# Twelve token tiles' output rows summed in DRAM, one tile's first-norm sums on ScalarE, and a new order of the work

## The chip, the cores and the metric

The kernel runs on one core of a Trainium2 chip. The metric is the time of one execution in device microseconds, the median of several runs. The core has five engines that run side by side and wait for each other by semaphores: PE (TensorE, matmuls into PSUM), DVE (VectorE), ACT (ScalarE), POOL (GpSimd) and SP (SyncE). SP issues most of the transfers, POOL those that accumulate into their destination.

## What is computed

The input x is A_q, 2048 tokens of 640 numbers in bf16. Two branches are mixed by a gate of one number for each token:

```python
g = sigmoid((x * gate_w).sum(-1, keepdims=True))
# branch A: a convolution over the whole sequence
kv = shift_conv(A_k, A_shift_k) * A_v          # four taps along the tokens
y  = causal_conv(kv, A_ssm_k) + kv * A_ssm_D    # by rfft and irfft of length 4096
a  = x * y
# branch B: a mixer and an MLP
h  = gelu(layernorm(x) @ w1)                    # 640 -> 640
hs = token_shift(h) @ w2                        # four groups, shifted by 1, -1, 2, -2 tokens
x1 = x + hs
b  = x1 + gelu(layernorm(x1) @ w3) @ w4         # 640 -> 1536 -> 640
out = g * a + (1 - g) * b
```

## The kernel before

All data stand in one SBUF array ("arena" in the profile), and PSUM is one array of eight banks ("PSall"). Tokens come in 16 tiles of 128 rows; X[:, t, :] holds tile t of x and is overwritten step by step until it holds (1 - g) * h2 @ w4.

*The first norm* (ln1, L892) has two forms. For tiles below LNS = 10, DVE makes the statistics with two bn_stats and one aggregate (ln_bn). For the others ACT makes them in two passes over the 640 columns, a sum and a sum of squares, each with an accumulated output. DVE normalises the tile, and PE (first 8 tiles) or a DMA transposes it.

*Mixer and MLP.* mm1 and mm2 are the two products of the mixer; the residual of mm2 is added on DVE (L967), which frees the PSUM bank, and ACT squares the result for the second norm. mm3 makes the MLP's hidden layer 512 tokens at a time (sc = 0 to 3), and mm4(t) (L993) its output for one tile: 12 matmuls of 384 columns and 12 of 256, and then an identity matmul that adds X's last 256 columns.

*The convolution* goes over five chunks of 128 channels. Transforms along the sequence are matmuls with constant matrices, and unit(c) (L1004) multiplies the spectra: products and sums on DVE, some of the sums by accumulating transfers of POOL within SBUF, where the order's list ON says so. final(g, o, q, k) (L1025) transforms back and multiplies by g * x, for a pair k of token tiles (ta = 4o + q and tb = 4o + 3 - q) and a group of columns: group 0 is columns 0 to 383, group 1 columns 384 to 639. Pairs 0 to 7 are tiles (12, 15), (13, 14), (8, 11), (9, 10), (4, 7), (5, 6), (0, 3), (1, 2). Group 1 needs units 3 and 4, which are the last ones.

*How the output comes together.* Columns 0 to 383 (NA = 384) are summed in DRAM: base(t) (L988) scales x by 1 - g on ACT and SP writes it; mm4(t) scales its result on ACT, and POOL adds it to DRAM with an accumulating transfer (L1000); group 0 of final is added in the same way (L1047), one transfer of 256 rows of 768 bytes for a pair. Columns 384 to 639 are summed on the chip: the identity matmul adds x in mm4, group 1 of final multiplies (L1050), adds X (L1051), and SP writes the sum, 256 rows of 512 bytes (L1053); pairs 6 and 7 do this in two halves. Since transfers to the same rows must follow one another, POOL waits for the landing of one before it issues the next to the same place.

*The order.* Each operation is recorded with a number, in the order of the calls, and SEQUENCE gives the order in which they are handed out to the engines; each engine runs its own operations strictly in that order. PLACES names the PSUM bank of each accumulation, and a bank's next user waits for the last reader of the one before. The semaphore waits follow from both lists. At the end SP waits for every transfer that it hasn't seen land.

Of the kernel before, what the change touches and what calls it, by code (L numbers as in the profile page):

```python
# [433 lines left out]
def bass_gated_mix__ssm_conv_h3__mixer_s_mlp__prompt_kernel(  # L434
    nc, A_q, A_k, A_v, A_shift_k, A_ssm_k, A_ssm_D, B_x, B_w1, B_w2, B_w3, B_w4, gate_w, out,
):
    S, D, F = 2048, 640, 1536
    NT, DC, FC, NB = 16, 5, 12, 4
    GROUPS = ((0, 3), (3, 5))
    NA = 384  # L440
# [28 lines left out]
    def ps(n, cls):  # L469
# [3 lines left out]
    SEQUENCE = [27, 46, 2, 4, 1, 7, 45, 0, 5, 24, 3, 8, 47, 25, 48, 28, 9, 130, 26, 10, 11, 31, 53, 12, 52, 32, 13,  # L473
# [383 lines left out]
    def bn_math(t0, t1):  # L857
        for a, b in ((t0, t1),) if t0 >= 4 else ((t, t + 1) for t in range(t0, t1)):
            mean, var = bna[:, a:b, 0], bna[:, a:b, 1]
            if a >= LNS:  # L860
                tt(st[0, 4][:, a:b], mean, mean, ALU.mult)
                stt(st[0, 3][:, a:b], st[0, 1][:, a:b], 1e-5, st[0, 4][:, a:b], ALU.add, ALU.subtract)
            else:
                ts(st[0, 3][:, a:b], var, 1e-5, None, ALU.add)
# [286 lines left out]
```

## Time and profile before

| | before |
|---|---|
| median of 3 runs | 222.24 us (221.77 to 222.59) |
| the profiled execution | 222.23 us |
| its span | 220.3 us |
| PE busy | 209.6 us (95%), 1410 matmuls |
| DVE busy | 211.6 us (96%), 417 instructions |
| ACT busy | 193.2 us (88%), 324 instructions |
| POOL busy | 55.9 us (25%), 57 instructions |
| DMA queue of SP | 66.2% of 16 engines' span |
| DMA queue of POOL | 27.7% of 16 engines' span |

Span is the time from the first instruction of the profiled execution to its last. Busy PE counts matmuls in flight, which overlap. A line of the profile can be that of a helper: L646 is every tensor_tensor on DVE, L651 every tensor_scalar, L656 every operation of ACT, L678 every matmul, L237 every DMA. Idle time stands in brackets behind an instruction, with what ended it. The landing of a transfer is counted from its issue.

### The profile page before, as it was taken

To read this page: it belongs to the slowest core of one execution; us is meant where nothing else is said; L and a number is where in the kernel's file an instruction comes from. 1 tells how busy PE (TensorE), PEld (TensorE's weight loads), DVE (VectorE), ACT (ScalarE), POOL (GpSimd) and SP (SyncE) were. 2 spreads that over 40 slices of the span, in tenths; PEclk is the share of its full clock that TensorE was granted. 3 is DMA by queue.
4 is the path that set the end of the run, shared out by engine and by line. 5 is a ranking of instruction groups with operands and counts; after the bars stand their busy time and mean duration, and the time that the engine had idled before them with its cause. 6 is when DMAs were issued, how large, how long until landed. Compare 5 with 4: busy or idle time off the path is not lost.

```text
span 220.3 us, 3850 instructions
## 1 busy us (share of the span) xinstructions
PE 209.6 (95%) x1410; PEld 125.9 (57%) x1410; DVE 211.6 (96%) x417; ACT 193.2 (88%) x324; POOL 55.9 (25%) x57
## 2 busy tenths in 40 slices
PE   5999999899999999999999999999999999999970
PEld 2489865455675444765446575445667445677740
DVE  5999999999999979999999999999999999999993
ACT  2389999999999999999999999999977898566981
POOL 0432303300005100005140002054025427277431
PEclk9999999999999999999999999999999999999996
DMA  6997999999998999959979885699699969889896
GB/s 168 348 283 183 216 201 271 175 247 201 161 338 227 269 257 183 206 98 184 215 139 148 190 153 95 129 167 195 139 226 147 218 119 254 179 100 96 110 158 118
DMA packets 80561, 41.39 MB, mean 188 GB/s; under 512 B 59129, under 2 KB 77086, under 8 KB 80542
## 3 DMA queue, kind: packets, MB, share of 16 engines
q1 hardware_dynamic: 73872, 31.89, 66.2%
q0 software_dynamic: 6496, 9.18, 27.7%
q8 instruction: 11, 0.18, 0.3%
q10 hardware_dynamic: 174, 0.07, 0.1%
q14 instruction: 8, 0.07, 0.1%
HBM read 14.88 MB, written 5.77 MB: 94 GB/s over the span
## 4 chain that ended last, share of the span: by engine, by line
DVE 73%; DMA 10%; PE 10%; ACT 3%; issue 2%; SPq 0%
DVE arena L646 63%; PE PSall L678 10%; DMA arena<-arena 8%; DVE arena L847 3%; DVE arena L651 3%; ACT arena L656 3%; DVE arena L967 2%; DMA arena<-in_A_q_dram 2%; DVE arena L933 1%; DVE arena L848 0%; DVE arena L852 0%; SPq L237 0%; DVE arena L721 0%
## 5 line engine op out<-in xcount | busy, mean ns | idle before, releaser
L678 PE MATMUL PSall<-arena 128*128 128x512 bf16 (+5 forms) x1349 | 201.3, 310 | 3.3 <-DVE arena L646 2.0
L646 DVE TENSOR_TENSOR arena<-arena 128x1024 bf16<-128x1024 bf16 (+12 forms) x266 | 173.4, 716 | 2.0 <-DMA arena<-arena 1.1
L678 PEld LDWEIGHTS PSall<-arena 128*128 128x128 bf16 x1349 | 121.7, 98 | 82.4 <-DVE arena L646 2.9
L656 ACT ACTIVATE arena<-PSall 128x512 bf16<-128x512 f32 (+6 forms) x157 | 93.1, 664 | 11.0 <-PE PSall L736 4.9
L656 ACT ACTIVATE arena<-arena 128x640 bf16<-128x640 bf16 (+5 forms) x105 | 90.4, 890 | 2.1 <-DVE arena L646 1.8
L855 POOL TENSOR_TENSOR arena<-arena 128x2 f32<-128x2 f32 (+2 forms) x15 | 19.5, 1306 | 84.1 <-DVE arena L852 67.9
L237 POOL DMA_DIRECT2D out_dram<-arena x24 | 25.5, 1302 | 15.5 <-DVE arena L646 8.5
L656 ACT ACTIVATE arena<-PSall,arena 128x640 bf16<-128x640 f32 (+2 forms) x32 | 20.5, 657 | 8.6 <-PE PSall L678 8.6
L237 POOL DMA_DIRECT2D arena<-arena x14 | 12.3, 882 | 59.6 <-DVE arena L646 59.6
L651 DVE TENSOR_SCALAR arena<-arena 128x640 bf16<-128x640 bf16 (+6 forms) x37 | 13.2, 378 | 0.1
L967 DVE SCALAR_TENSOR_TENSOR arena<-PSall,arena 128x640 bf16<-128x640 f32 x16 | 12.7, 812 | 0.0
L847 DVE BATCH_NORM_STATS2 arena<-arena 128x6 f32<-128x320 bf16 x20 | 8.7, 478 | 1.8 <-DMA arena<-in_A_q_dram 1.8
L701 PE MATMUL PSall<-arena 128*128 128x512 bf16 x15 | 6.4, 589 | 2.2 <-DVE arena L698 2.2
L933 DVE TENSOR_SCALAR arena<-arena 32x256 bf16<-32x256 bf16 (+1 forms) x23 | 5.5, 237 | 0.3
L656 ACT ACTIVATION_READ_ACCUMULATOR arena<-arena 128x1 f32 x28 | 5.7, 204 | 0.0
L701 PEld LDWEIGHTS PSall<-arena 128*128 128x128 bf16 x15 | 1.8, 134 | 5.0 <-issue 2.8
L908 PE MATMUL PSall<-arena 128*128 128x128 bf16 x40 | 3.4, 220 | 0.2 <-DVE arena L651 0.2
L852 DVE SCALAR_TENSOR_TENSOR arena<-arena 128x2 f32<-128x2 f32 (+2 forms) x19 | 3.0, 159 | 0.0
L908 PEld LDWEIGHTS PSall<-arena 128*128 128x128 bf16 x40 | 2.4, 98 | 0.9 <-DVE arena L651 0.9
L704 ACT ACT_TABLE_LOAD x1 | 1.3, 1283 | 1.4 <-PEq L1136 1.4
L848 DVE BATCH_NORM_AGGREGATE arena<-arena 128x2 f32<-128x12 f32 x10 | 1.8, 199 | 0.0
L967 DVE DVE_READ_ACCUMULATOR arena<-PSall,arena 128x1 f32 x16 | 1.2, 76 | 0.0
(19 smaller groups left out, 2.9 us busy)
## 6 DMA issues: line engine op xcount, KB each, us to landing
arena<-arena POOLq DMA_DIRECT2D x9, 512.0 KB, 6.9
arena<-in_A_ssm_k_dram SPq DMA_DIRECT2D x5, 512.0 KB, 4.5
arena<-in_A_q_dram SPq DMA_DIRECT2D x6, 320.0 KB, 5.9
arena<-in_B_w_dram SPq DMA_DIRECT2D x1, 1920.0 KB, 14.0
out_dram<-arena SPq DMA_DIRECT2D x16, 96.0 KB, 2.9
out_dram<-arena POOLq DMA_DIRECT2D x16, 96.0 KB, 4.7
arena<-in_A_q_dram SPq DMA_DIRECT2D x8, 192.0 KB, 3.3
out_dram<-arena POOLq DMA_DIRECT2D x8, 192.0 KB, 4.4
```

What stands on the lines that cost most here:

```text
L237: fn = lambda e: e.dma_start(out, in_, **kw)
L646: P.op(eng, lambda e: e.tensor_tensor(o, real(a), real(b), op), [a, b], [o], dve_ns(o, [a, b], 2) if eng == "dve" else 500)
L651: P.op(eng, lambda e: e.tensor_scalar(o, real(a), s1, s2, op0=op0, **({} if op1 is None else {"op1": op1})), [a] + aps, [o], dve_ns(o, [a] ...
L656: P.op("act", lambda e: e.activation(real(o), real(a), f, bias=bias, scale=scale, **({"accum_out": accum} if accum is not None else {})), ...
L678: fns.append(lambda e, l=l, r=r, i=i: e.matmul(real(o), l, r, start=(i == 0), stop=(i == last)))
L701: P.op("pe", lambda e: e.matmul(real(pw), warm[:, 0:128], warm[:, 128:640], start=True, stop=True), [warm], [pw], 427.0 if i < 14 else 216.0)
L847: P.op("dve", lambda e, o=o, i=i: e.bn_stats(o, i), [i], [o], 400)
L852: P.op("dve", lambda e: e.scalar_tensor_tensor(o, a, x, b, op0=op0, op1=op1), [a, b] + aps, [o], n_of(o) / 0.96 + 65)
L855: P.op("pool", lambda g: g.tensor_tensor(o, a, e, ALU.pow), [a, e], [o], dur)
L908: P.op("pe", [lambda e, c=c, pb=pb, xn=xn: e.transpose(real(pb)[:, 128 * c:128 * (c + 1)], xn[:, 128 * c:128 * (c + 1)], ident) for c in r ...
L933: P.op("dve", lambda e, o=hT[q, 4, c0:c0 + n], i=hx[q, :]: e.tensor_scalar(o, i, 1.0, None, op0=ALU.mult), [hx[q, :], *near], [hT[q, 4, c0 ...
L967: P.op("dve", lambda e: e.scalar_tensor_tensor(x, real(pr), 1.0, x, op0=ALU.mult, op1=ALU.add, accum_out=st[1, 0][:, t:t + 1]), [pr, x], [ ...
```

## The change

DRAM_PAIRS names pairs 0 to 5, that is tiles 4 to 15. For these, all 640 columns are summed in DRAM: base scales and writes 640 columns in place of 384, mm4 drops the identity matmul and its accumulating transfer has 640 columns, and group 1 of final drops the addition of X; its product goes to DRAM by an accumulating transfer of POOL where SP wrote the sum before. Tiles 0 to 3 (pairs 6 and 7) stay as they are. POOL so has six transfers more and SP six fewer, and the bytes that POOL adds for twelve tiles of mm4 grow by two thirds.

In the first norm, tile 3 joins tiles 10 to 15, whose sums ACT makes. Its two bn_stats, its aggregate and one small operation on DVE become two passes on ACT and two small operations on DVE.

SEQUENCE and PLACES are new. Beside the operations that come and go, SP's and POOL's own orders stay; on PE 8, on ACT 21 and on DVE 31 operations stand elsewhere in their engine's list. On DVE the read of mm2 for tile 5 comes eight places earlier, and one product of unit 0, which feeds that unit's first accumulating transfer, stands four places earlier, ahead of an addition of the shift convolution and the read of mm2 for tile 12. In POOL's list the new transfers stand near the end: behind group 0 of pair 1 come group 1 of pair 2, group 0 of pairs 5 and 7, group 1 of pairs 3, 0, 5 and 1, group 0 of pair 6, and group 1 of pair 4. The last nine operations of DVE behind the product for that last transfer belong to pairs 6 and 7.

```diff
-            if a >= LNS:
+            if a in ON_ACT:
                 tt(st[0, 4][:, a:b], mean, mean, ALU.mult)
...
-    PET, LNS, LNA = 8, 10, 4
+    PET, LNA = 8, 4
+    ON_ACT = (3, 10, 11, 12, 13, 14, 15)
 
     def ln1(t0, t1):
         for t in range(t0, t1):
-            if t < LNS:
+            if t not in ON_ACT:
                 ln_bn(t, X[:, t, :])
                 continue
...
+    DRAM_PAIRS = (0, 1, 2, 3, 4, 5, )
+    n_out = [NA] * NT
+    for k in DRAM_PAIRS:
+        n_out[12 - 4 * (k // 2) + k % 2] = n_out[15 - 4 * (k // 2) - k % 2] = D
+
     def base(t):
-        x = X[:, t, 0:NA]
+        x = X[:, t, 0:n_out[t]]
         scale(x, x, gst[4][:, t:t + 1], True)
-        P.dma(sp, out[0, 128 * t:128 * (t + 1), 0:NA], x)
+        P.dma(sp, out[0, 128 * t:128 * (t + 1), 0:n_out[t]], x)
...
-               ([(ident, X[:, t, lo:hi])] if lo else []))
+               ([(ident, X[:, t, lo:hi])] if hi > n_out[t] else []))
         act(X[:, t, :], pr[:, 512 - NA:512 - NA + D], ACTF.Copy, scale=gst[4][:, t:t + 1])
-        P.dma("pool", out[0, 128 * t:128 * (t + 1), 0:NA], X[:, t, 0:NA], accum=True)
+        P.dma("pool", out[0, 128 * t:128 * (t + 1), 0:n_out[t]], X[:, t, 0:n_out[t]], accum=True)
...
-        if not g:
+        if not g or k in DRAM_PAIRS:
             tt(gy, gy, qt, ALU.mult)
-            P.dma("pool", rows(out, 0, n), gy, accum=True)
+            P.dma("pool", rows(out, 128 * c0, n), gy, accum=True)
             return
```

More of the change, by code (lines that the diff above doesn't have):

```diff
@@ L471, in ps @@
         return v if n == 1 else v.rearrange("p (b n) -> p b n", b=2)
-    SEQUENCE = [27, 46, 2, 4, 1, 7, 45, 0, 5, 24, 3, 8, 47, 25, 48, 28, 9, 130, 26, 10, 11, 31, 53, 12, 52, 32, 13,
[59 rows of a table removed]
-    PLACES = [2, 4, 7, 0, 4, 5, 6, 1, 2, 1, 3, 4, 2, 3, 3, 4, 2, 6, 7, 2, 0, 4, 5, 7, 6, 2, 6, 1, 0, 7, 4, 1, 6, 0,
[2 rows of a table removed]
+    SEQUENCE = [46, 27, 2, 4, 1, 7, 45, 0, 5, 24, 3, 8, 47, 25, 48, 28, 9, 130, 10, 26, 53, 11, 31, 52, 12, 32, 49,
[59 rows of a table added]
+    PLACES = [2, 4, 7, 0, 6, 5, 6, 1, 2, 1, 3, 4, 2, 3, 3, 4, 2, 6, 7, 2, 5, 4, 1, 4, 6, 2, 0, 1, 0, 7, 4, 7, 6, 0,
[2 rows of a table added]
                 0, 7, 2, 2, 1, 3, 4, 2, 3, 5, 4, 4, 0, 6, 0, 2, 6, 6, 4, 0, 0, 2, 2, 4, 0, 6, 6, 3, 5, 1, 4, 4, 5,
[2 rows of a table removed]
[2 rows of a table added]
                 7, 2, 5, 4, 0, 6, 2]
```

126 rows, old and new, of tables (PLACES, SEQUENCE) are left out of this document.

## The prediction, made before the result was known

> **What bounds the kernel now.** I read the groups by line first, then the engines' busy time by stretch of the span, then the end of the chain of waits beside the POOL and SP transfers. Two rows of the page, and the busy time by stretch (start:end, length, then PE, PEld, DVE, ACT, POOL with counts, clock, DMA share, GB/s):
>
> ```profile
> L678 PE MATMUL PSall<-arena 128*128 128x512 bf16 (+5 forms) x1349 | 201.3, 310 | 3.3 <-DVE arena L646 2.0
> L646 DVE TENSOR_TENSOR arena<-arena 128x1024 bf16<-128x1024 bf16 (+12 forms) x266 | 173.4, 716 | 2.0 <-DMA arena<-arena 1.1
> ...
> 40.00:97.00 57.00, 57.00 (x358) 32.33 (x357) 55.49 (x105) 55.76 (x86) 5.16 (x4) 1.00 1.04 222
> 97.00:165.00 68.00, 68.00 (x393) 38.12 (x392) 67.86 (x96) 65.40 (x88) 15.60 (x14) 1.00 0.85 161
> 165.00:201.00 36.00, 36.00 (x226) 21.91 (x225) 35.58 (x52) 27.12 (x47) 18.57 (x20) 1.00 0.98 164
> 201.00:210.00 9.00, 9.00 (x71) 6.55 (x70) 8.96 (x25) 8.63 (x18) 4.93 (x5) 1.00 0.83 100
> 210.00:217.10 7.10, 3.88 (x29) 2.37 (x26) 7.03 (x27) 5.22 (x11) 1.94 (x2) 0.93 0.99 151
> ```
>
> From 40 to 201 us three engines are full at once: PE without a gap, DVE with 2.07 us of idle (1.51 + 0.14 + 0.42), ACT with 3.84 us of idle up to 165 (1.24 + 2.60) and loose only after it. Time taken from one of them there moves the end only as far as the other two can follow. In the last stretch it is DVE (7.03 of 7.10). The end, from the chain of waits (start, length, what), the POOL and SP timelines, and landings of single issues (last number: us from issue to landing; the SP row is the issue at 217.39, the POOL row that at 214.25):
>
> ```profile
> 206.48 4.25 DVE arena L646 x15
> ...
> 216.80 0.29 DVE arena L646
> ```
> ```profile
> 195.11 2.98 POOL L237 DMA_DIRECT2D out_dram<-arena  x3 [1.20 <-ACT arena L656]
> 198.34 2.11 POOL L237 DMA_DIRECT2D out_dram<-arena  x2 [0.25 <-DMA out_dram<-arena]
> 202.01 2.09 POOL L237 DMA_DIRECT2D out_dram<-arena  x2 [1.56 <-ACT arena L656]
> 205.14 1.20 POOL L237 DMA_DIRECT2D out_dram<-arena  x1 [1.04 <-DMA out_dram<-arena]
> 208.27 2.47 POOL L237 DMA_DIRECT2D out_dram<-arena  x2 [1.93 <-DVE arena L646]
> 214.25 1.19 POOL L237 DMA_DIRECT2D out_dram<-arena  x1 [3.50 <-DVE arena L646]
> ```
> ```profile
> 217.39 0.43 SPq L237 DMA_DIRECT2D out_dram<-arena  x1
> ...
> out_dram<-arena SPq DMA_DIRECT2D x1, 64.0 KB, 2.0
> ...
> out_dram<-arena POOLq DMA_DIRECT2D x1, 192.0 KB, 4.2
> ```
>
> DVE stops at 217.09, the last SP write lands at 217.39 + 2.0 = 219.4, and the span closes 0.9 later at 220.3. POOL has long pauses, and its last transfer lands at 214.25 + 4.2 = 218.4, a microsecond before SP's. The profiled execution took 222.23 us, 1.93 above its span; the median of the runs shown is 222.24, so a sum on this trace carries over as it is.
>
> **Tile 3's sums on ScalarE.** DVE loses two bn_stats and one aggregate and gains one small operation; ACT gains two 640-wide passes with their accumulator reads.
>
> ```profile
> 6.05 1.67 DVE L847 BATCH_NORM_STATS2 arena<-arena 128x6 f32<-128x320 bf16 x4 [0.88 <-DMA arena<-in_A_q_dram]
> 7.64 0.19 DVE L848 BATCH_NORM_AGGREGATE arena<-arena 128x2 f32<-128x12 f32 x1
> ...
> 11.42 1.67 DVE L847 BATCH_NORM_STATS2 arena<-arena 128x6 f32<-128x320 bf16 x4
> ```
> ```profile
> 4.19 0.87 SPq L237 DMA_DIRECT2D arena<-in_A_q_dram  x1
> ...
> arena<-in_A_q_dram SPq DMA_DIRECT2D x1, 320.0 KB, 6.9
> ...
> 7.72 0.18 ACT L656 ACTIVATE arena<-PSall 128x10 bf16<-128x10 f32 x1 [4.87 <-PE PSall L736]
> 8.69 0.70 ACT L656 ACTIVATE arena<-PSall 128x640 bf16<-128x640 bf16 x1 [0.80 <-PE PSall L908]
> ```
>
> Two bn_stats are half of 1.67, the aggregate adds about what the new small operation costs: DVE is 0.8 us ahead by 8 us. It doesn't keep that. The statistics of tiles 6 and 7 start at 11.42, and their load, issued at 4.19, lands at 11.1; so 0.3 us is kept. The ACT passes (about 0.81 + 0.2 us each) fall into the idle times of 4.87 and 0.80 us, and cost nothing; without that cover they would be 2.0 us.
>
> **The identity matmuls.** Twelve mm4 lose their 128x256 matmul.
>
> ```profile
> L678 PE MATMUL PSall<-arena 128*128 128x384 bf16 x50 | 8.8, 326 | 0.0
> L678 PE MATMUL PSall<-arena 128*128 128x256 bf16 x52 | 6.3, 273 | 0.0
> ```
>
> These are the matmuls between 187.1 and 200.7, back to back: 50 x 384 + 52 x 256 columns in 13.6 us, so 256 columns take 0.107 us. Twelve are 1.3 us of PE, real on an engine without a gap, but worth what DVE and ACT can follow.
>
> **The wider base scalings.** Twelve go from 384 to 640 columns.
>
> ```profile
> L656 ACT ACTIVATE arena<-arena 128x640 bf16<-128x640 bf16 x44 | 34.9, 808 | 0.0
> L656 ACT ACTIVATE arena<-arena 128x384 bf16<-128x384 bf16 x24 | 14.6, 614 | 0.0
> ```
>
> That is 0.19 us each, 2.3 us in all; ten stand before 165, 1.9 us of new work against 3.84 us of idle there. The other two fall where ACT is loose.
>
> **The new order.** Two moves are aimed at waits that the trace shows.
>
> ```profile
> 39.47 2.84 PE L678 MATMUL PSall<-arena 128*128 128x1 bf16 x30 [0.88 <-DVE arena L967]
> ...
> 69.03 1.22 DVE L646 TENSOR_TENSOR arena<-arena 128x2048 bf16<-128x2048 bf16 x1
> ...
> 70.57 1.07 POOL L237 DMA_DIRECT2D arena<-arena  x1 [1.33 <-DVE arena L646]
> ...
> 80.56 7.57 DVE L646 TENSOR_TENSOR arena<-arena 128x2048 bf16<-128x2048 bf16 x12 [1.12 <-DMA arena<-arena]
> ```
>
> PE's 0.88 us is a PSUM bank that mm2 of tile 5 frees on DVE; that read moves eight places up in DVE's list, so the wait goes. DVE's 1.12 us is the accumulating transfer issued at 70.57; the product before it (69.03) moves ahead of two operations, which brings the issue forward by up to 2 us. I let that wait go too.
>
> So the work reaches the tail earlier by 0.3 + 1.1 on DVE, less what ACT can't follow. The lower bound is -0.5 (1.4 less the whole 1.9 of new ACT work), the upper 2.4 (0.3 and all of DVE's 2.07 idle gone). I take 1.2, near the two waits that have a row, with 0.2 off for ACT because it has twice the idle that it needs.
>
> **The tail.** Six pairs of tiles (0 to 5) lose the addition of X and give their 128x512 product to POOL in place of SP.
>
> ```profile
> L646 DVE TENSOR_TENSOR arena<-arena 128x512 bf16<-128x512 bf16 x12 | 4.9, 426 | 0.0
> ```
>
> Of these twelve in the tail six go: 6 x 0.43, some 2.0 to 2.6 us of DVE. This would be the gain if DVE ended the kernel. But POOL's list of the tail grows from four to ten transfers: after group 0 of pair 1 come group 1 of pair 2, group 0 of 5 and 7, group 1 of 3, 0, 5 and 1, group 0 of 6, group 1 of 4. That is nine of 256 rows each. The issue of one costs POOL 1.2 us (the rows of one at 205.14 and 214.25; the two at 208.27 take 2.47). The first can't start before pair 2's product, which now runs from 206.48 to 206.91; the way from DVE to a POOL issue is 0.3 us (70.25 to 70.57), so 207.2, and 206.0 with the 1.2 gained. The ninth, of pair 4, would start at 206.0 + 8 x 1.22 = 215.8. Its product doesn't hold it up: nine operations of about 0.3 us stand behind it in DVE's list, so even with DVE's old end it is ready by 214.6. The ninth lands 4.2 later, at 220.0. Before, the last landing was at 219.4. SP, which has only pairs 6 and 7 left, would be done by about 217.
>
> Sum: 220.0 + 0.9 + 1.93 = **222.8 us**, 0.6 above the time before. What DVE, PE and ACT save is paid back by a queue that had been idle.
>
> The pace is the open cost, since the trace has no accumulating transfer of 512-byte rows and no burst of 256-row ones. Downward, 128 rows cost POOL 0.88 (the burst at 195.11 is two of 128 rows and one of 256: 2.98 less 1.22, halved). Upward, two 256-row transfers that follow each other, issued at 196.24 and 198.34, landed 4.6 and 4.4 later, 1.85 apart. I take 1.22, because the descriptors are as many and the queue itself can be quicker:
>
> ```profile
> 165.42 3.01 POOL L237 DMA_DIRECT2D out_dram<-arena  x3
> ...
> out_dram<-arena POOLq DMA_DIRECT2D x3, 96.0 KB, 7.2
> ```
>
> These three, issued 0.54 us apart behind a slow one, all landed 7.2 later: a queue with descriptors waiting moves 128 rows in 0.54 us.
>
> The landing is bounded by the 4.2 of 192 KB in 256 rows and, below, by 128 rows of 96 KB that found the queue empty at 202.0:
>
> ```profile
> out_dram<-arena POOLq DMA_DIRECT2D x1, 96.0 KB, 2.8
> ```
>
> Half the rows is further off than two thirds of the bytes, so I keep 4.2; with 2.8 the sum is 221.4.
>
> **Rivals.**
> *The other products set the end (faster).* If POOL issues these at the 0.88 of a 128-row transfer, the ninth lands at 206.0 + 7.0 + 4.2 = 217.2, beside SP's last; the time is 217.2 + 0.9 + 1.93 = 220.0. For it: starts within a burst lie 0.54 apart. Against it: each 256-row row of the timeline.
> *The accumulating queue becomes the bound (slower).* Its place is the same tail; it decides once a 256-row transfer takes the 16 engines longer than the 1.22 of its issue. Eight more at 1.4 to 1.85 after the first landing (206.0 + 4.4) end at 221.6 to 225.2; the middle gives 226.2. For it: the 1.85 above, and this row of 195 to 200, five transfers in 5 us:
>
> ```profile
> q0 software_dynamic: 646, 0.45, 90.7%
> ```
>
> Against it: the 0.54 of a filled queue.
> *ACT eats the advance (slower).* If its 1.9 us can't use the idle, which is mostly waits for PE, the gain is -0.5 in place of 1.2: 224.5. For it: ACT is 96% full up to 165. Against it: it gets twice the room it needs.
>
> *Short landings (faster).* If the bytes alone set how long a transfer takes beyond a fixed part, the rows here (96 KB 2.8, 192 KB 4.2) put 128 KB at 3.3, and the time at 221.9; a smaller fixed part would be needed to go below 221.1. The Trainium skill, DMA: Bandwidth & Descriptors, section Anatomy of one DMA, gives one: a POOL transfer is 2.0 us plus its bytes at 436 GB/s, an estimated 2.3 us here, and a sum of 220.9. The trace disagrees, with 4.2 for 192 KB.
>
> **Chances and range.** This measurement can't tell less than about 0.5%, 1.1 us, from no change. POOL's issues set the end: 0.48, own range 221.6 to 224.5 (advance 2.4 to -0.5). The faster rival 0.23, short landings 0.03, the queue 0.13, ACT 0.13. Faster: 0.23 and 0.03; same: 0.37 of the first and 0.02 of ACT; slower: the rest, 0.35. The range 220.0 to 225.6 leaves out about half of the first rival's case below and half of the queue's above.
>
> **What would show it.** If right: nine POOL issues from about 206 without a pause, 1.2 us apart; DVE's last operation near 214, several us before the last landing; the last landing POOL's, not SP's; DVE's wait at 80 us gone; PE without a gap from about 38.5. If landings lag further and further behind the issues, it is the queue; if DVE or PE waits for ACT between 97 and 165, the ACT rival. It is wrong if POOL pauses in the tail, or if SP's last write is the last to land.

## The result and the profile after

The changed kernel takes 232.90 us, median of 4 runs (232.20 to 233.22), against 222.04 (221.77 to 222.59) before: a ratio of 1.047, 95% interval 1.0431 to 1.0509. The profiled execution took 232.2 us with a span of 230.4. The forecast was 222.8, with a range up to 225.6; the change is slower by far more than that range allows.

The first view is the page's groups by line of the changed kernel, the two rows that were read before the change.

```profile
L678 PE MATMUL PSall<-arena 128*128 128x512 bf16 (+5 forms) x1337 | 202.5, 312 | 9.1 <-DMA arena<-arena 6.3
L646 DVE TENSOR_TENSOR arena<-arena 128x1024 bf16<-128x1024 bf16 (+12 forms) x261 | 172.1, 718 | 10.0 <-ACT arena L656 9.1
```

The matmuls waited 3.3 us in all before the change and now wait 9.1, of which 6.3 are for a transfer within SBUF. The additions and products of DVE are fewer and no slower, but wait 10.0 us in place of 2.0. The second view is the busy time by stretch, in the columns of the prediction's table.

```profile
40.00:97.00 57.00, 56.24 (x350) 31.63 (x346) 55.64 (x105) 55.60 (x85) 5.93 (x4) 1.00 1.03 221
97.00:165.00 68.00, 68.00 (x393) 38.30 (x392) 67.86 (x93) 66.35 (x89) 16.94 (x16) 1.00 0.86 164
165.00:201.00 36.00, 30.39 (x165) 16.34 (x163) 28.54 (x43) 23.28 (x38) 12.14 (x14) 0.91 0.95 176
201.00:210.00 9.00, 9.00 (x70) 6.69 (x69) 8.74 (x14) 7.02 (x14) 6.67 (x7) 1.00 1.03 118
210.00:217.10 7.10, 7.10 (x57) 5.16 (x55) 6.68 (x23) 6.75 (x15) 4.86 (x6) 1.00 0.93 102
217.10:226.00 8.90, 3.19 (x23) 2.00 (x21) 5.49 (x20) 4.29 (x10) 7.83 (x7) 0.77 1.21 138
```

Up to 165 us little has changed. The loss is in the third row: PE does 30.39 of 36 us where it did 36.00, and at a mean granted clock of 0.91. The chain of waits of the changed kernel (start, length, what) names the place:

```profile
149.88 13.67 PE PSall L678 x88
163.56 0.02 issue
163.58 0.66 ACT arena L656
164.24 12.03 DMA arena<-arena
176.27 0.05 issue
176.31 24.32 PE PSall L678 x122
```

The PE timeline of that place before, and then after:

```profile
168.82 11.40 PE L678 MATMUL PSall<-arena 128*128 128x256 bf16 x58
```
```profile
168.81 1.89 PE L678 MATMUL PSall<-arena 128*128 128x512 bf16 x8
176.31 3.92 PE L678 MATMUL PSall<-arena 128*128 128x512 bf16 x9 [5.61 <-DMA arena<-arena]
```

After the change PE stands still for 5.61 us, until a transfer lands that SP issued at 164.24 and that took 12.03. It is the DMA transpose of the second norm's output for tiles 12 and 13 (in ln2), which mm3 of the last 512 tokens reads. The landing rows of that one issue, before and then after (last number: us from issue to landing):

```profile
arena<-arena SPq DMA_TRANSPOSE x1, 7.1
```
```profile
arena<-arena SPq DMA_TRANSPOSE x1, 12.0
```

Before, it was issued at 163.34 and landed at 170.4, 1.3 us before PE needed it. The timelines of SP and then of POOL, before:

```profile
156.36 1.71 SPq L234 DMA_TRANSPOSE arena<-arena  x1
...
159.91 5.77 SPq L234 DMA_TRANSPOSE arena<-arena  x2
```
```profile
161.24 0.86 POOL L237 DMA_DIRECT2D arena<-arena  x1 [9.18 <-DVE arena L646]
164.89 0.86 POOL L237 DMA_DIRECT2D arena<-arena  x1 [2.79 <-DVE arena L646]
```
The same two after:

```profile
157.35 1.71 SPq L234 DMA_TRANSPOSE arena<-arena  x1
...
160.91 8.41 SPq L234 DMA_TRANSPOSE arena<-arena  x2
```
```profile
159.89 0.86 POOL L237 DMA_DIRECT2D arena<-arena  x1 [8.57 <-DVE arena L646]
163.55 0.86 POOL L237 DMA_DIRECT2D arena<-arena  x1 [2.79 <-DVE arena L646]
```

SP's three transposes (of kv of channel chunk 4, of tiles 14 and 15, of tiles 12 and 13) start 0.9 to 1.0 us later, and POOL's two accumulating transfers of unit 3, 512 KB each, 1.35 us earlier. The last transpose was issued before the second of POOL's and is now issued after it. The queues' rows (packets, MB, share of the 16 engines) tell what follows; q0 is POOL's, q1 SP's. Before, from 165.75 to 169:

```profile
q1 hardware_dynamic: 1189, 0.30, 115.2%
q0 software_dynamic: 16, 0.01, 3.4%
```

After, from 166.5 to 170 and, in the second fence, from 170 to 176.3:

```profile
q0 software_dynamic: 156, 0.52, 96.4%
q1 hardware_dynamic: 138, 0.03, 6.3%
```
```profile
q0 software_dynamic: 528, 0.61, 80.5%
q1 hardware_dynamic: 1286, 0.35, 48.5%
```

Before, the transpose had the engines to itself, though POOL's second sum had been issued at 164.89. After, it has a few per cent of them while unit 3's sum moves. While mm4's transfers of tiles 7, 6 and 10, issued right behind that sum, move beside it, SP's queue has somewhat over a third of what moves.

The cause of this delay stands in the order on DVE. kv ends with two operations (the sum and the difference of the halves, 0.68 us each) that release its transpose. In the changed list three operations of units 3 and 2, of 1.22 and twice 0.69 us, stand ahead of these two. SP issues in its order, so the second norm's first transpose is late with kv's, and its issue falls beside unit 3's first sum. The time that SP spends on the issue of a transpose (min/median/max in ns), before and then after:

```profile
L234 SPq DMA_TRANSPOSE arena<-arena x3: 1477/1712/2342, 156.4 to 163.3; - x3
```
```profile
L234 SPq DMA_TRANSPOSE arena<-arena x3: 1714/3284/5087, 157.4 to 164.2; - x3
```

Before, the shortest is that of tiles 14 and 15, and SP is free again at 161.39, 2 us before it issues the last. After, this one takes 3.28 us, until 164.20, and the last follows at once: now it is SP that holds it up. POOL's sums are not early because of the three operations. Where these alone are moved, in the kernel before, POOL's first sum is issued at 161.54; where kv stands ahead in the changed kernel, at 160.28. All of DVE is ahead there, by the rest of the new order.

PE's loss is more than its wait. Its granted clock (the number behind POOL's count) in stretches of 2 us:

```profile
172.00:174.00 2.00, 0.00 (x0) 0.00 (x0) 1.97 (x4) 0.73 (x1) 0.74 (x1) 1.00 1.30 145
174.00:176.00 2.00, 0.00 (x0) 0.00 (x0) 1.13 (x3) 0.00 (x0) 0.00 (x0) 0.53 1.39 134
176.00:178.00 2.00, 1.69 (x5) 0.59 (x6) 0.00 (x0) 0.00 (x0) 0.00 (x0) 0.50 1.14 236
178.00:180.00 2.00, 2.00 (x6) 0.75 (x5) 0.00 (x0) 0.48 (x1) 0.00 (x0) 0.50 0.96 254
180.00:182.00 2.00, 2.00 (x8) 0.84 (x7) 0.41 (x1) 2.00 (x4) 0.00 (x0) 0.76 0.00 1
182.00:184.00 2.00, 2.00 (x11) 0.94 (x10) 2.00 (x3) 1.64 (x4) 0.86 (x1) 1.00 0.00 0
```

From 176.31 to about 181.0 (0.76 over two us is 1.0 us at half clock) PE runs at half its clock, which by this reckoning costs 2.3 us. Together with the wait that is 7.9 us.

### The profile page after: what moved, and what is told of

Its sections match the earlier page's. It is cut to its first block, busy times and chain, and to the rows that moved or that the text cites. A ratio compares the mean times of both kernels' runs of the same rounds, so it can differ in the third digit from the quotient of the medians.

```text
span 230.4 us, 3822 instructions
## 1 busy us (share of the span) xinstructions
PE 210.5 (91%) x1398; PEld 125.8 (55%) x1398; DVE 209.8 (91%) x409; ACT 196.9 (85%) x328; POOL 64.0 (28%) x63
## 4 chain that ended last, share of the span: by engine, by line
PE 64%; DMA 12%; DVE 8%; POOL 5%; ACT 3%; issue 2%; SPq 2%; POOLq 1%
PE PSall L678 64%; DMA arena<-arena 7%; POOL out_dram L237 5%; DVE arena L646 4%; DMA out_dram<-arena 3%; ACT arena L656 3%; DMA arena<-in_A_q_dram 3%; DVE arena L968 2%; DVE arena L651 2%; SPq L237 2%; DVE arena L847 1%; DVE arena L934 1%; POOLq L1127 1%; PE PSall L909 0%; DVE arena L852 0%
## 5 line engine op out<-in xcount | busy, mean ns | idle before, releaser
L678 PE MATMUL PSall<-arena 128*128 128x512 bf16 (+5 forms) x1337 | 202.5, 312 | 9.1 <-DMA arena<-arena 6.3
L646 DVE TENSOR_TENSOR arena<-arena 128x1024 bf16<-128x1024 bf16 (+12 forms) x261 | 172.1, 718 | 10.0 <-ACT arena L656 9.1
L678 PEld LDWEIGHTS PSall<-arena 128*128 128x128 bf16 x1337 | 121.5, 98 | 89.7 <-DMA arena<-arena 7.4
L656 ACT ACTIVATE arena<-PSall 128x512 bf16<-128x512 f32 (+7 forms) x157 | 92.6, 649 | 13.8 <-PE PSall L678 12.4
L656 ACT ACTIVATE arena<-arena 128x640 bf16<-128x640 bf16 (+5 forms) x107 | 93.5, 904 | 3.5 <-DMA arena<-in_A_q_dram 3.2
L855 POOL TENSOR_TENSOR arena<-arena 128x2 f32<-128x2 f32 (+2 forms) x15 | 20.1, 1345 | 81.7 <-DVE arena L852 67.3
L237 POOL DMA_DIRECT2D out_dram<-arena x30 | 32.9, 1667 | 11.2 <-ACT arena L656 5.5
L847 DVE BATCH_NORM_STATS2 arena<-arena 128x6 f32<-128x320 bf16 x18 | 8.0, 480 | 1.3 <-DMA arena<-in_A_q_dram 1.1
L852 DVE SCALAR_TENSOR_TENSOR arena<-arena 128x2 f32<-128x2 f32 (+3 forms) x20 | 3.1, 157 | 0.2 <-ACT arena L656 0.2
```

The lines of the kernel that those rows point to most:

```text
L237: fn = lambda e: e.dma_start(out, in_, **kw)
L646: P.op(eng, lambda e: e.tensor_tensor(o, real(a), real(b), op), [a, b], [o], dve_ns(o, [a, b], 2) if eng == "dve" else 500)
L656: P.op("act", lambda e: e.activation(real(o), real(a), f, bias=bias, scale=scale, **({"accum_out": accum} if accum is not None else {})), ...
L678: fns.append(lambda e, l=l, r=r, i=i: e.matmul(real(o), l, r, start=(i == 0), stop=(i == last)))
L847: P.op("dve", lambda e, o=o, i=i: e.bn_stats(o, i), [i], [o], 400)
L852: P.op("dve", lambda e: e.scalar_tensor_tensor(o, a, x, b, op0=op0, op1=op1), [a, b] + aps, [o], n_of(o) / 0.96 + 65)
```

## The experiments

Times are medians, beside the kernel before on the same chip: 221.90 for the first four, 222.21 for the next four, 222.02 for the three after them, 221.87 for the last. The numbers of operations in SEQUENCE are those of the changed kernel: 766, 762 and 761 are the three operations of units 3 and 2, 707 and 708 the last two of kv. The lists are laid out on more lines in these kernels, so a line of the program has a higher number in their profiles: the matmuls of L678 are L690, DVE's L646 is L658.

**kv's two operations ahead again.** The one move undone in the changed kernel.

```diff
-  766, 718, 762, 929, 1012, 761, 1023, 708, 719, 763, 707,
+  707, 708, 766, 718, 762, 929, 1012, 761, 1023, 719, 763,
```

> The changed kernel with one move in its list of operations: the two VectorE operations of kv of channel group 4, which release SP's transposes, stand again ahead of three operations of units 3 and 2, as before the change. Theory (order): the 5.6 us in which PE stands still at 170 come from the second-norm transpose of tiles 12 and 13, which reaches the DMA engines behind POOL's accumulating transfers of unit 3, because kv's two operations were moved back. Then the transpose is issued about 2 us earlier, lands by 171, PE has no gap over 1 us there, and the time is 226.5 to 228.5. Rival (width): the transfers of mm4 with 1280-byte rows in place of 768 hold up the transpose whatever the order; then it lands after 174 all the same and the time stays over 231.

225.01 us (224.61 to 225.76), ratio 1.0146 (1.0118 to 1.0174). The transpose, issued at 163.32, lands in 6.5 us:

```profile
arena<-arena SPq DMA_TRANSPOSE x1, 6.5
```

PE has no wait on a transfer there, and the median falls by 7.9 us (7.1 between the two profiled executions, 232.2 and 225.08). That is about all that PE had lost, and more than the expectation, which counted only the wait and not the clock. The wide transfers are still there, so they don't hold up the transpose by themselves.

**The new order without any pair summed in DRAM.**

```diff
-    DRAM_PAIRS = (0, 1, 2, 3, 4, 5, )
+    DRAM_PAIRS = ()
```

> The changed kernel's order and its tile 3 on ScalarE, but no pair summed in DRAM: the scalings and mm4's transfers are 384 columns wide again, the identity matmuls are back, and the six products of group 1 get their addition on VectorE and go out by SP, at the places where POOL's transfers stood. Theory (order): the stall at 170 stays, somewhat shorter since the rows are narrower (3.5 to 5.5 us), and the tail is the old one; 224.5 to 227. Rival (width): no stall, 220.5 to 222.

227.99 us, ratio 1.0268 (1.0229 to 1.0307). The stall is there with narrow transfers, 3.1 us long:

```profile
PE PSall L690 <- DMA arena<-arena: 3.1, 1, 3.1
```

So the order makes the stall; with the six pairs it is longer, 5.6 us. Part of that is the wider rows (the transpose lands 12.0 us after its issue and not 10.7), part is that PE gets there 0.8 us earlier in the changed kernel. The time is above what was expected; this order loses some 2 us at the end when nothing is summed in DRAM (below, 224.04).

**The six pairs in the old order.** The same edit of the data flow, in the order of before, tile 3 on DVE.

> The order of before with the six pairs summed in DRAM (wide scalings, wide transfers, no identity matmul, POOL's transfer in the place of SP's write); tile 3 stays on VectorE. Theory (order): the transpose of tiles 12 and 13 lands by 171.5, no gap of PE over 1 us between 165 and 180; only the tail costs: POOL's nine transfers 1.22 apart from about 207, the last landing about 14.4 after the first issue, the span's end 2 later, so 225 to 227. Rival (width): the stall of PE is here too, 3 us or more, and the time over 229. Rival (tail costs nothing): 222 or less.

226.00 us, ratio 1.0187 (1.0166 to 1.0208): as the theory has it, no stall, and 4.1 us that are left for the six pairs, mostly at the end of the kernel (the ninth transfer of the tail lands at 222.2). On the same chip the new order with kv ahead took 225.01, 1.0 us less, and its nine transfers start at 206.76 in place of 207.63.

**Two wide transfers out of the way.** mm4's transfers of tiles 7 and 6 (889 and 883) go ahead of unit 3's first sum (768) in POOL's list.

```diff
-  768, 720, ..., 773, ..., 889, ..., 883,
+  889, 883, 768, 720, ..., 773,
```

> The changed kernel with two of POOL's transfers moved: the sums of mm4 of tiles 7 and 6 (1280-byte rows) are issued ahead of the first sum of unit 3, at about 152, where the DMA engines are idle. Theory (order): unit 3's second sum, 512 KB, still stands ahead of the transpose; it lands at 172 to 174.5 and PE waits 2 to 4 us; 229 to 231.5. Rival (width): two of the three wide transfers are out of the way, the transpose lands by 171.5, PE's wait is under 1 us, 226.5 to 228.

228.65 us (227.62 to 229.45), ratio 1.0318 (1.0286 to 1.0350). The transpose lands at 173.9 and PE waits 2.4 us, both as the theory expected, since unit 3's second sum still stands ahead. Against what the expectation says, the DMA engines weren't idle at 152: their share is 0.99 from 152 to 154. The time is a little under its range. In the profiled run, of 227.62 us, the clock stayed at 1.00 through this shorter wait; the other three took 0.9 to 1.8 us longer, at mean granted clocks of 0.975 to 0.980 in place of 0.988.

**The move alone, in the kernel before.**

```diff
-  707, 718, 708, 929, 696, 766, 709, 1012, 719, 762, 1023, 922, 761,
+  766, 762, 761, 707, 718, 708, 929, 696, 709, 1012, 719, 1023, 922,
```

> The kernel before with one move: three VectorE operations of units 3 and 2 (a product of 2048 columns and two of 1024, 2.6 us) stand ahead of kv's two operations of channel group 4, as in the changed kernel; all else is as before. Theory (order): the transposes of kv and of the second norm are issued about 2.6 us later (kv's at about 159 in place of 156.4), unit 3's second sum is on the DMA engines ahead of that of tiles 12 and 13, PE stands still for 3 to 6 us after 170, and the time is 225.5 to 229. Rival (the whole new order, or ScalarE's work, makes the stall): no gap over 1 us, 221.5 to 223.

227.64 us, ratio 1.0266 (1.0221 to 1.0311). Three operations of 2.6 us, moved past two on the same engine, cost 5.4 us. The last transpose is issued at 165.79, behind POOL's second sum at 165.20, and the PE timeline shows the same wait at the same place:

```profile
176.01 4.37 PE L690 MATMUL PSall<-arena 128*128 128x512 bf16 x13 [3.79 <-DMA arena<-arena]
```

**Fewer pairs, in the new order with kv ahead.** DRAM_PAIRS is empty, (0, 2, 3) or (0, 1, 2, 3).

> The changed kernel's order with kv's two operations ahead again and tile 3 on ScalarE, no pair summed in DRAM. Theory (the advance of 1.2 us is real, and only the stall and the tail cost time): 220.4 to 221.6, faster than before. Rival (the advance is lost at the end): 221.7 to 223.

> The same, with three pairs (0, 2, 3) summed in DRAM and three (1, 4, 5) by VectorE and SP: six of POOL's transfers of 256 rows in the tail in place of nine. Theory (POOL's issues of 1.22 us are the tail's price): the last of them lands about 3.7 us sooner than with six pairs, so VectorE and SP set the end; 220.0 to 222. Rival (the price is one of the sums in DRAM before the tail, wide scalings and wide transfers): 223 to 225, half way between none and six pairs.

> The same, with four pairs (0 to 3) summed in DRAM: seven of POOL's transfers of 256 rows in the tail. Theory (POOL's issues): two fewer than with six pairs, 2.4 us less than 225.0: 222 to 223. Rival (work before the tail): 223.8 to 225.

No pair: 224.04, ratio 1.0089 (1.0065 to 1.0113). Three: 222.10, ratio 1.0000 (0.9982 to 1.0017). Four: 223.16, ratio 1.0046 (1.0030 to 1.0062). With six it was 225.01. From three pairs upwards a pair costs about 1.0 us, somewhat under the 1.22 of an issue on POOL; three are at the edge of what was expected, and four above the theory's range by 0.2. The first expectation failed: the new order without pairs is slower than before. Its waits from 200 us on, and those of before, show PE waiting for DVE twice as long:

```profile
PE PSall L690 <- DVE arena L658: 3.9, 5, 2.0
```
```profile
PE PSall L678 <- DVE arena L646: 2.0, 3, 1.0
```

**Old order at the end.** Three pairs in the order of before; then the new order (kv ahead) up to 163 us and the old one behind it, with three pairs and with none.

> The kernel before with only the first three products of the tail (pairs 0, 2 and 3) summed in DRAM, and its own order; tile 3 on VectorE. Theory (VectorE sets the end of the tail as long as POOL has few transfers there): three additions of 0.43 us and six identity matmuls of 0.107 are gone, POOL's six transfers fit, its last starts near 213 and its closing follows 1.84 after the landing; 220.9 to 222. Rival (each pair costs the same, by the ladder from six pairs in this order): 224.

> The changed order with kv's two operations ahead up to the transpose of tiles 12 and 13 (163 us), and from there the order of before; tile 3 on ScalarE; pairs 0, 2 and 3 summed in DRAM. Theory (the new order is worth 0.5 to 1.0 us up to 163, and the old one is the better tail): 220.2 to 221.5, faster than before. Rival (the advance does not reach the end): equal to the same with the old order throughout, 221 to 222.2.

> The same mixed order and no pair summed in DRAM. Theory (the 2 us that the new order lost without pairs are lost after 163, in places laid for POOL's transfers): 221 to 222.2, some 2 us less than 224.0. Rival (the loss stems from before 163): 223.3 to 224.5.

Old order, three pairs: 222.69, ratio 1.0035 (1.0018 to 1.0051). Mixed, three pairs: 222.37, ratio 1.0012 (0.9996 to 1.0028). Mixed, no pair: 222.27, ratio 1.0002 (0.9989 to 1.0015). The first two miss: in no order do three pairs beat the kernel before. The third comes out at its edge, and says that the 1.8 us of the order without pairs were lost after 163 us; that they were lost in the places laid for POOL's transfers is the expectation's reading, and wasn't tried by itself. No kernel of the study beats the one before.

**Unit 3's sums on DVE.** The changed kernel in its own order, kv behind; two bits of ON are cleared, so that DVE makes the two sums of unit 3 that POOL's transfers made.

```diff
-    ... 1010001101" "001000010100 ...
+    ... 1010001100" "000000010100 ...
```

> The changed kernel, in its own order, with two sums of unit 3 (the accumulating transfers of 512 KB that POOL issued at 159.9 and 163.6) done by VectorE, as two additions of 1.22 us at the same places; mm4's wide transfers then no longer queue behind them and go out at about 151. The transposes are released as late as in the changed kernel (kv's issued at about 157.4). Theory (sharing: the transpose of tiles 12 and 13 is slow because accumulating transfers move on the same DMA engines): it lands by 169.5, PE no longer waits for it, VectorE is 2.4 us later instead; 226.5 to 230. Rival (late issue alone): it lands after 173 and PE waits for it as before; 232 or more.

227.37 us, ratio 1.0233 (1.0211 to 1.0255). The second norm's two transposes are issued at 161.68 and 163.70 (160.91 and 164.24 in the changed kernel, 159.91 and 163.34 before), and land by 169.3. The row of the second norm's two, with the median of their landings:

```profile
arena<-arena SPq DMA_TRANSPOSE x2, 5.3
```

PE doesn't wait for a transfer, and the time is 225.0 and the 2.4 us that DVE now works more. Issued 0.4 us later than before the change, the last transpose lands 1.1 us earlier. It is not the late issue by itself that delays the transpose, but the accumulating transfers beside it: unit 3's sums and what follows them in POOL's list, which are out of the way together here.

## Why the prediction was wrong

**The new order.** This is the step that failed. It counted the two waits at which moves were aimed, and took 1.2 us of advance, with -0.5 as its lower bound. It didn't follow the other operations on DVE that change places to what they release on SP's queue, and so left out the wait that came of it. Putting three operations of units 3 and 2 ahead of kv's last two cost 7.9 us here, as undoing it showed, and 5.4 in the kernel before. The neighbours of the transpose were in the trace: it landed at 170.4 for a matmul at 171.75. With the stall undone the time, 225.01, lies inside the forecast's range, though above the 221.6 to 224.5 of its main case.

Nor did the advance come where it was counted. DVE's wait at 80 us went, but ACT's took part of its place (0.51 at 89.94). PE's 0.88 at 39.47 went, and a wait for a transfer came, with another of 0.5 for ACT:

```profile
47.04 50.22 PE L678 MATMUL PSall<-arena 128*128 128x1 bf16 x303 [0.66 <-DMA arena<-arena]
```

So PE won little by the exchange. With the stall undone, the first product of the tail reached POOL at 206.76, 0.4 us earlier than the 207.2 of the forecast's sum and not 1.2. But 207.2 was itself too early: in the old order with the same six pairs it is 207.63. Against that the new order, with tile 3's sums on ACT, is 0.9 us ahead, and 1.0 in the time (225.01 and 226.00). So where POOL ends the kernel, most of the advance is there. Where it doesn't, nothing of it shows at the end: the mixed order without pairs takes as long as the kernel before.

**The tail.** This part was right in its mechanism. Where the stall is undone, POOL's timeline reads

```profile
204.81 1.20 POOL L237 DMA_DIRECT2D out_dram<-arena  x1 [2.09 <-DMA out_dram<-arena]
206.76 10.97 POOL L237 DMA_DIRECT2D out_dram<-arena  x9 [0.75 <-DVE arena L658]
```

Nine issues in 10.97 us are 1.22 each, the value taken. In the changed kernel they start at 213.95 and take the same 10.97:

```profile
213.95 10.97 POOL L237 DMA_DIRECT2D out_dram<-arena  x9 [0.35 <-DVE arena L646]
```

Beside the start, two terms of the sum were mis-sized. The ninth landed 4.7 us after its turn on POOL began (216.5 to 221.2), not 4.2. And the span ended 2.1 us after the last landing, not 0.9. With the measured terms, 206.76 + 8 x 1.22 + 4.7 + 2.1 + 1.8 (from the span to the run) is 225.1; 225.01 was measured. This sum is 2.3 us over the forecast's: 0.76 for the later start, 0.5 of landing and 1.2 of closing, less 0.13 from the span to the run.

**The edits costed at nothing** cost nothing that shows: from 97 to 165 PE and DVE are as full as before (68.00 and 67.86) with the wide scalings on ACT. Tile 3's sums and the identity matmuls weren't tried alone.

**The rivals.** None of them is what happened. Other products setting the end failed, as POOL's transfer lands last. The accumulating queue is hardly a bound: in the changed kernel a landing came 2.8 to 3.9 us after the end of its own turn on POOL, from the first of the nine to the last, without growing. Where the stall is undone this lag grew by 1.1 us, from 2.4 to 3.5: landings 1.36 us apart behind issues 1.22 apart, where the rival had 1.4 to 1.85. ACT ate nothing between 97 and 165. Short landings failed: where the stall is undone the first of the nine took 3.6 us from its turn on POOL and the ninth 4.7, and the rival had 3.3 or less. The list of signs had the right one, "PE without a gap from about 38.5", and it is the one that the trace contradicts.

## What to carry to other kernels

When an operation moves in one engine's list, ask for each operation that it passes what that one releases on other engines, and what runs on the DMA engines at that time: here two additions of 0.68 us held a chain of three transposes, and a slip of 1 us behind a 512 KB transfer became 7.9 us. A transfer of small packets that others wait for belongs ahead of one of large packets, not beside it. An idle queue isn't free capacity: its price is the pace of its issues, its landing and the closing behind it, counted to the end of the kernel. A gain on one of several full engines is a gain only if the others have it too.

## What the runs showed of the hardware

*Two queues on the same 16 engines don't share them evenly.* From 166.5 to 170 us, with both queues filled, POOL's sum in SBUF had 96.4% and SP's transpose 6.3%, as quoted above. The Trainium skill, DMA: Bandwidth & Descriptors, section Queues, rings and completion order, says that each engine takes turns between its queues, a packet at a time. The trace agrees, and the turns account for the shares: 156 packets of POOL's moved beside 138 of SP's, nearly one for one. By the two rows (a share of 16 engines over 3.5 us, divided by the packets) one of POOL's took about 0.35 us and one of SP's 0.03; in the packet records the first are of 4 KB, the second of 256 bytes. What turns don't tell is the case before: POOL's second sum, issued at 164.89, moved next to nothing until the transpose was through (16 packets beside 1189). Why is open.

*PE's clock fell with the stall.* After waits of 3.1, 3.8 and 5.6 us the clock stood at 0.50, and it came back 2.7 to 4.7 us after PE's return; a wait of 2.4 us left it at 1.00 in the run that was profiled. The Trainium skill, TensorE: Matmul & The Clock Gate, Part 1, gives some 3.4 us of idleness for the fall and as much work for the return. The runs agree roughly: the shortest wait after which it fell is 3.1 us, and there it fell 2.3 us after PE's last matmul (from 171.52 to 173.86, in the changed kernel without pairs), in the other two 3.3 and 3.4 us after it.

*The kernel closes later when POOL's transfers land late.* SP's last wait is on the closing that all engines share. In the changed kernel it is the first of these rows (1.7 us as well with kv ahead, and with six pairs in the old order), before the change the second:

```profile
SPq L1127 <- PEq L1127: 1.7, 1, 1.7
```
```profile
SPq L1121 <- PEq L1121: 0.2, 1, 0.2
```

In the traces of all fourteen kernels POOL's closing instruction ends 1.60 to 1.84 us after POOL's last landing: at 223.06 with the landing at 221.22 where kv stands ahead, at 220.02 with 218.42 before. SP is through 0.3 to 0.8 us after the last landing that it waits for. Before, the two met within 0.12 us, so that it couldn't be seen. With four pairs, POOL's last transfer lands at 219.68 and SP's at 220.22, and still it is POOL's closing, at 221.44, that the end of the span (221.67) follows. That POOL's closing waits for its transfers is read from these times and wasn't tried by itself.
